# Blocks of half-height matmuls: three pairs side by side instead of two, with the order of VectorE's work changed around them

## The chip, the cores and the metric

One core of one Trainium2 chip. The time is the device time of one execution in microseconds (us), the median of several. Engines: PE is TensorE's matmul, DVE is VectorE, ACT is ScalarE, POOL is GpSimd, SPq is the queue of SyncE that issues the DMAs. "Before" is the tuned kernel, "changed" is the kernel with the change.

## The reference

Two branches read the same normalised input (2048 rows of 448 features), and the output joins them:

```python
def attn(x, wqkv, wo):                 # 16 heads of 28; each row sees 8 rows, 2 apart
    qkv = x @ wqkv
    idx = pos[:, None] - arange(8) * 2
    logits = (q * k[idx]).sum(-1) * 28 ** -0.5       # masked where idx < 0
    return (softmax(logits) * v[idx]).sum() @ wo
def ffn(x, w1, b1, w2, b2):            # 448 -> 1792 -> 448
    return gelu_tanh(x @ w1 + b1) @ w2 + b2
xn  = layernorm(x)
out = x + attn(xn) * silu(ffn(xn))
```

## The kernel before

The rows are worked in four chunks of 512. 448 features are three full contractions of 128 and a "rest" of 64. Two rests, in the upper and the lower 64 rows of the array, run together (0.22 us for the two in the trace of this kernel, as much as one full matmul takes there), so the work comes in pairs: six full matmuls, then two rests (or the rests first). The pairs are seven of the first feed-forward layer (`ps_h`, k = 0 to 6) and four of q/k (`ps_qk`, g = 0 to 3) per chunk. Before, pairs alternate "full, rest" and "rest, full", so that the rests of two neighbours meet in one block:

```python
def ffn1(c, k, even):
    ps = ffn1_tiles(k)
    if even:
        ffn1_full(c, k, ps, True);  ffn1_rest(c, k, ps, False)
    else:
        ffn1_rest(c, k, ps, True);  ffn1_full(c, k, ps, False)
    return ps

def feed_forward_1(c, ps, wos):
    ...
    for k in range(1, MT // 2):
        if (c, k) in ((0, 6), (1, 4), (2, 4)):
            qk_pair(c + 1, 0, True, DD)            # q/k pair 0 of the next chunk
        ps = ffn1(c, k, not odd)
        gelu(k, ps)
        ...
        if k in ((3, 5, 6) if c == 3 else (4,)):   # output projections: ps_s, then sg and o_t on VectorE
            for _ in range(4 if c == 2 else 2):
                if wos: wo_job(wos.pop(0))
        if c and k in (3, 5):                      # tanh on ScalarE, then g on VectorE
            silu_job(4 * (c - 1) + k - 3)
            silu_job(4 * (c - 1) + k - 2)

def ln_apply(t):
    nc.vector.tensor_scalar(xnb[t % 4][:, 0:D], xt(t), mv[:, t, 0:1], rstd[:, t:t + 1], ...)
    nc.vector.tensor_copy(xnb[t % 4][:, D:512], xnb[t % 4][:, D - 64:D])   # doubled features
def ln_dma(t):                                     # tiles 4 to 15: transposed by DMA
    nc.sync.dma_start_transpose(xnT[:, :, LEAD + t * P:LEAD + (t + 1) * P], xnb[t % 4][:, :])
```

`mv` and `rstd` are the mean and the normalising factor of a tile of 128 rows, made from its statistics (`ln_stats`); `rstd` ends just before the tile can be normalised. Two PSUM pools rotate: `psA` (2 tiles of two banks) and `psB` (4 tiles of one bank, shared by q/k, v, `ps_h` of k = 0 and 3, `ps_y`, the output projections and the attention product `psO`). After a chunk's feed-forward pairs come the scores `S`, the other q/k pairs and `psO`, then four more attention units.

The softmax here doesn't subtract the row's maximum and nothing guards it: scores larger than these inputs give would overflow.

## Time and profile before

| | before |
|---|---|
| median (range) | 167.37 us (167.26 to 167.57), 3 runs |
| span of the profiled run | 165.6 us |
| PE, ACT, DVE busy | 158.9, 125.9, 112.9 us |
| stage of chunk 0, 1, 2, 3 | 18.65, 20.66, 22.18, 16.06 us |

A stage, here and below, is the time in PE's timeline from the first `ps_h` matmul of a chunk to the score group after that chunk's first `psO` (in chunk 3, to the next score group). The chain of waits lists pieces of work in order of time (start, length, engine, tile, line); two neighbouring PE pieces whose times join mean that PE never waited. The prediction shows the lines themselves.

### The profile page before, as it was taken

How to read it: one execution, taken by the hardware profiler on the slowest of the kernel's cores; microseconds unless marked ns; L12 is line 12 of the kernel's file. 1: busy time of each engine (PE TensorE's matmuls, PEld its weight loads, DVE VectorE, ACT ScalarE, POOL GpSimd, SP SyncE). 2: the span in 40 equal slices, each digit the busy share in tenths (PEclk: the TensorE clock that was granted, in tenths of full speed). 3: DMA queues.
4: the chain of work that ended last, by engine and by line, in shares of the span. 5: the costliest groups of instructions: out<-in, count | busy, mean ns of one | idle time of the engine just before them, and what ended most of it. 6: DMA issues, size and time to landing. Idle time of an engine off the chain costs nothing.

```text
span 165.6 us, 3242 instructions
## 1 busy us (share of the span) xinstructions
PE 158.9 (96%) x1290; PEld 71.8 (43%) x1301; DVE 112.9 (68%) x256; ACT 125.9 (76%) x198; POOL 4.5 (3%) x16
## 2 busy tenths in 40 slices
PE   6899999999999999999999999999999999999990
PEld 2343333345554334445554334335555334445570
DVE  5967890497888638687888308877777507678893
ACT  3773698598887795998887795698888698698830
POOL 7002000000000000000000000000000000000000
PEclk9999999999999999999999999999999999999999
DMA  5999995520111100100211100300000002020011
GB/s 134 302 306 267 325 190 93 164 44 4 32 36 32 32 0 4 55 0 0 36 32 32 36 0 0 112 1 4 0 4 0 0 0 60 31 83 0 4 55 55
DMA packets 15963, 10.62 MB, mean 64 GB/s; under 512 B 7500, under 2 KB 15948, under 8 KB 15948
## 3 DMA queue, kind: packets, MB, share of 16 engines
q1 hardware_dynamic: 15660, 10.18, 24.0%
q10 hardware_dynamic: 288, 0.23, 0.5%
q8 instruction: 10, 0.16, 0.4%
q14 instruction: 5, 0.04, 0.1%
HBM read 7.00 MB, written 1.84 MB: 53 GB/s over the span
## 4 chain that ended last, share of the span: by engine, by line
PE 83%; ACT 7%; DVE 5%; DMA 2%; issue 1%; DVEq 0%
PE ps_y L281 23%; PE ps_h L249 21%; PE ps_qk L197 11%; PE ps_v L228 8%; PE ps_s L331 6%; PE ps_h L258 4%; PE S L355 3%; PE psO L370 3%; ACT hT L264 3%; PE ps_qk L207 3%; DMA x<-in_A_x_dram 2%; ACT th L310 1%; DVE sg L337 1%; DVE st L161 1%; ACT L509 1%
## 5 line engine op out<-in xcount | busy, mean ns | idle before, releaser
L264 ACT ACTIVATE hT<-ps_h,b1f 128x512 bf16<-128x512 f32 x56 | 34.1, 695 | 10.1 <-PE ps_h L258 7.3
L249 PE MATMUL ps_h<-xnT,w 128*128 128x512 bf16 x161 | 39.3, 380 | 0.5 <-issue 0.2
L281 PE MATMUL ps_y<-w,hT 128*128 128x448 bf16 x196 | 39.5, 353 | 0.0
L361 ACT ACTIVATE E<-S 128x976 bf16<-128x976 f32 x34 | 31.6, 983 | 2.1 <-PE S L355 0.8
L281 PEld LDWEIGHTS <-hT 128*128 128x128 bf16 x196 | 18.0, 98 | 16.7
L249 PEld LDWEIGHTS <-w 128*128 128x128 bf16 x168 | 15.0, 98 | 22.1 <-issue 6.4
L363 DVE TENSOR_TENSOR E<-E,mk_gen 128x976 bf16<-128x976 bf16 x30 | 20.0, 666 | 6.7 <-ACT E L361 6.5
L197 PE MATMUL ps_qk<-xnT,wqk 128*128 128x512 bf16 x92 | 22.2, 380 | 0.3 <-issue 0.2
L379 DVE TENSOR_TENSOR oT<-psO,den 128x484 bf16<-128x484 f32 (+1 forms) x17 | 11.3, 662 | 10.1 <-ACT den L378 10.1
L214 DVE CAST qT<-ps_qk 128x512 bf16<-128x512 f32 x16 | 11.0, 687 | 9.5 <-PE ps_qk L207 8.4
L228 PE MATMUL ps_v<-wv,xnT 128*128 128x448 bf16 x68 | 15.7, 353 | 0.1
L311 DVE SCALAR_TENSOR_TENSOR g<-th,y 128x448 bf16<-128x448 bf16 x13 | 7.6, 621 | 10.8 <-ACT th L310 10.8
L337 DVE SCALAR_TENSOR_TENSOR sg<-ps_s,g 128x448 bf16<-128x448 f32 (+2 forms) x17 | 10.1, 592 | 7.0 <-PE ps_s L331 6.9
L233 ACT CAST vw<-ps_v 128x448 bf16<-128x448 f32 x17 | 9.1, 533 | 6.9 <-PE ps_v L228 6.8
L197 PEld LDWEIGHTS <-wqk 128*128 128x128 bf16 x96 | 8.9, 98 | 11.5 <-issue 1.8
L331 PE MATMUL ps_s<-wo,oT 128*128 128x448 bf16 (+2 forms) x68 | 13.4, 342 | 0.0
L377 ACT ACTIVATE den<-den 128x484 f32<-128x484 f32 (+1 forms) x17 | 10.3, 605 | 4.0 <-DVE den L374 4.0
L374 DVE STREAM_SHUFFLE den<-psO 128x484 f32<-128x484 f32 (+1 forms) x17 | 11.7, 695 | 0.0
L378 ACT ACTIVATE den<-den 128x484 f32<-128x484 f32 (+1 forms) x17 | 10.3, 606 | 0.5
L161 DVE BATCH_NORM_STATS2 st<-x 128x6 f32<-128x448 bf16 x16 | 9.8, 610 | 0.9 <-DMA x<-in_A_x_dram 0.8
L331 PEld LDWEIGHTS <-oT 128*128 128x128 bf16 x68 | 6.4, 98 | 5.9 <-issue 0.2
L228 PEld LDWEIGHTS <-xnT 128*128 128x128 bf16 x68 | 6.3, 98 | 6.0 <-ACT xnT L181 0.6
(71 smaller groups left out, 139.8 us busy)
## 6 DMA issues: line engine op xcount, KB each, us to landing
out_dram<-o_t SPq DMA_DIRECT2D x15, 112.0 KB
w<-in_B_w_dram SPq DMA_DIRECT2D x1, 1568.0 KB
x<-in_A_x_dram SPq DMA_DIRECT2D x3, 448.0 KB
w<-in_B_w_dram SPq DMA_DIRECT2D x2, 672.0 KB
wraw<-in_A_wqkv_dram SPq DMA_DIRECT2D x1, 672.0 KB
w<-in_B_w_dram SPq DMA_DIRECT2D x4, 112.0 KB
wo<-in_A_wo_dram SPq DMA_DIRECT2D x16, 24.5 KB
wv<-in_A_wqkv_dram SPq DMA_DIRECT2D x1, 336.0 KB
```

Source lines behind the costliest of these rows:

```text
L161: nc.vector.bn_stats(out=st[:], in_=xt(t))
L197: nc.tensor.matmul(ps[w][:, :], wqk[:, kt, 16 * w + 4 * g:16 * w + 4 * g + 4, :], xnT[:, kt, LEAD + c * CH:LEAD + (c + 1) * CH], start=(fi ...
L228: nc.tensor.matmul(ps[:, :], xnT[:, kt, o:o + P], wv[:, kt, :], start=(kt == 0), stop=(kt == KT - 1))
L249: nc.tensor.matmul(ps[i][:, :], w1[:, kt, m * P:(m + 1) * P], xnT[:, kt, LEAD + c * CH:LEAD + (c + 1) * CH], start=(first and kt == 0), st ...
L264: nc.scalar.activation(hT[:, m, :], ps[i][:, :], ACT.Gelu_apprx_tanh, bias=b1f[:, m:m + 1])
L281: nc.tensor.matmul(ps[:, :], hT[:, m, tt * P:(tt + 1) * P], w2[:, m, :], start=(m == 0), stop=(m == MT - 1))
L331: nc.tensor.matmul(ps[:, 0:n], oT[:, g, t * P:(t + 1) * P], wo[:, g, cs], start=(g == 0), stop=(g == 3))
L337: nc.vector.scalar_tensor_tensor(out=sg[:, cs], in0=ps[:, 0:cs.stop - cs.start], scalar=0.5, in1=g_sb[t % NG][:, cs], op0=ALU.mult, op1=AL ...
L361: nc.scalar.activation(ev, Sp[p2][:, :, :, 0:QW], ACT.Exp, scale=SCALE)
L363: nc.vector.tensor_tensor(out=ev, in0=ev, in1=mkb, op=ALU.mult)
L374: nc.vector.stream_shuffle(den[:, :, 0:n], psO[:, :, 0:n], [0] * 32)
L379: nc.vector.tensor_tensor(out=oT[:, :, QB * b:QB * b + n], in0=psO[:, :, 0:n], in1=den[:, :, 0:n], op=ALU.mult)
```

## The change

The intent: fewer blocks of rests, since every block costs PE time on entry and exit (about 0.10 us each in the trace of the kernel before; "mode changes" below). Rests of up to three pairs stand side by side where the PSUM banks allow it, the doubled features of the first chunk are made by two 64-wide transposes in the array instead of a copy on VectorE, and one of the last additions goes to GpSimd. The diff is shortened.

```diff
+    def group(*jobs):
+        for job in jobs: job.alloc()
+        jobs[0].full(True)
+        jobs[0].rest(False)
+        for job in jobs[1:]: job.rest(True)
+        jobs[0].done(True)
+        for job in jobs[1:]:
+            job.full(False)
+            job.done(False)
 ...
+        p = [FF1(c, 0, ahead=gelus), FF1(c, 1, then=stats(4 * c + 8)), FF1(c, 2),
+             FF1(c, 3, then=...silus(t)...), FF1(c, 4), FF1(c, 5, then=silus(t + 2)), FF1(c, 6, ...)]
+        group(*p[0:3])
+        if c == 3:
+            group(*p[3:5]); wo_jobs(2); group(*p[5:7]); wo_jobs(4)
+        elif c:
+            group(p[3], *q0)
+            group(*p[4:6])          # ends with tanh and g of k = 5
+            wo_jobs(4)              # 2 projections in chunk 1, 4 in chunk 2
+            group(p[6], *last)      # last = q/k pair 1, and S with q/k pair 2
+        else:
+            group(*p[3:5]); group(p[5], *q0); group(p[6], *last)
 ...
-        for kt in range(KT):
+        for kt in range(3):
             nc.tensor.transpose(pT[:, kt, :], xnb[t % 4][:, kt * P:(kt + 1) * P], ident[:])
+        for r in (0, 64):
+            nc.tensor.transpose(pT[r:r + 64, 3, :], xnb[t % 4][:, D - 64:D], ident[:])
 ...
-        for g in range(4):                     # chunk 0: statistics of tile 4 + g after pair g
-            qk_pair(0, g, g % 2 == 0, DA) ...
+        group(QK(0, 0, DA), QK(0, 1, DA))
+        ln_stats(4); ln_stats(5)
+        group(QK(0, 2, DA), QK(0, 3, DA))
+        ln_stats(6); ln_stats(7)
 ...
-        wo_put(14, s14)
+        wo_put(14, s14, add=nc.gpsimd)
```

Besides, in the start part, v blocks 1 and 3 go to `psA`, the evacuations of the transposes go ahead of those of v, and ten warming matmuls run instead of nine.

More of the change, by code (lines that the diff above doesn't have):

```diff
@@ L166, in ln_rstd, with ln_apply @@
         nc.scalar.activation(rstd[:, t0:t0 + n], lnv[:, t0:t0 + n], ACT.Exp, scale=-0.5)
-    def ln_apply(t):
+    def ln_apply(t, double=True):
         nc.vector.tensor_scalar(xnb[t % 4][:, 0:D], xt(t), mv[:, t, 0:1], rstd[:, t:t + 1],
                                 op0=ALU.subtract, op1=ALU.mult)
-        nc.vector.tensor_copy(xnb[t % 4][:, D:512], xnb[t % 4][:, D - 64:D])
+        if double:
+            nc.vector.tensor_copy(xnb[t % 4][:, D:512], xnb[t % 4][:, D - 64:D])
     def ln_tr(t):
         pT = psB.tile([P, KT, P], BF16, name="pT", tag="B")
-        for kt in range(KT):
+        for kt in range(3):
             nc.tensor.transpose(pT[:, kt, :], xnb[t % 4][:, kt * P:(kt + 1) * P], ident[:])
+        for r in (0, 64):
+            nc.tensor.transpose(pT[r:r + 64, 3, :], xnb[t % 4][:, D - 64:D], ident[:])
         return pT
@@ L192, in qk_weights @@
                               bass.AP(src.tensor, src.offset, [list(src.ap[0]), [DH, H], [1, 32]]))
-    def qk_full(c, g, ps, first, copies):
-        for w in range(2):
-            for kt in range(3):
-                nc.tensor.matmul(ps[w][:, :], wqk[:, kt, 16 * w + 4 * g:16 * w + 4 * g + 4, :],
-                                 xnT[:, kt, LEAD + c * CH:LEAD + (c + 1) * CH],
-                                 start=(first and kt == 0), stop=(not first and kt == 2))
-            if not first:
-                qk_put(c, g, w, ps, copies)
@@ L203, in qk_rest, with __init__, alloc, full @@
-    def qk_rest(c, g, ps, first, copies):
-        for w in range(2):
-            r = slice(64 * w, 64 * w + 64)
-            nc.tensor.matmul(ps[w][:, :], wqk[r, 3, 16 * w + 4 * g:16 * w + 4 * g + 4, :],
-                             xnT[r, 3, LEAD + c * CH:LEAD + (c + 1) * CH], start=first, stop=not first)
-        if not first:
-            for w in range(2):
-                qk_put(c, g, w, ps, copies)
     def qk_put(c, g, w, ps, copies):
         copies[w]((qT, kT)[w][:, g, LEAD + c * CH:LEAD + (c + 1) * CH], ps[w][:, :])
-    def qk_pair(c, g, even, copies):
-        ps = [psB.tile([P, CH], F32, name="ps_qk", tag="B") for _ in range(2)]
-        for f in ((qk_full, qk_rest), (qk_rest, qk_full))[not even]:
-            f(c, g, ps, f is (qk_full, qk_rest)[not even], copies)
+    class QK:
+        def __init__(self, c, g, copies):
+            self.c, self.g, self.copies = c, g, copies
+        def alloc(self):
+            self.ps = [psB.tile([P, CH], F32, name="ps_qk", tag="B") for _ in range(2)]
+        def full(self, first):
+            c, g = self.c, self.g
+            for w in range(2):
+                for kt in range(3):
+                    nc.tensor.matmul(self.ps[w][:, :], wqk[:, kt, 16 * w + 4 * g:16 * w + 4 * g + 4, :],
+                                     xnT[:, kt, LEAD + c * CH:LEAD + (c + 1) * CH],
+                                     start=(first and kt == 0), stop=(not first and kt == 2))
+                if not first:
+                    qk_put(c, g, w, self.ps, self.copies)
+        def rest(self, first):
+            c, g = self.c, self.g
+            for w in range(2):
+                r = slice(64 * w, 64 * w + 64)
+                nc.tensor.matmul(self.ps[w][:, :], wqk[r, 3, 16 * w + 4 * g:16 * w + 4 * g + 4, :],
+                                 xnT[r, 3, LEAD + c * CH:LEAD + (c + 1) * CH], start=first, stop=not first)
+        def done(self, first):
+            if first:
+                for w in range(2):
+                    qk_put(self.c, self.g, w, self.ps, self.copies)
@@ L222, with v_mm @@
+    def group(*jobs):
+        for job in jobs:
+            job.alloc()
+        jobs[0].full(True)
+        jobs[0].rest(False)
+        for job in jobs[1:]:
+            job.rest(True)
+        jobs[0].done(True)
+        for job in jobs[1:]:
+            job.full(False)
+            job.done(False)
     DA, DD = (nc.vector.tensor_copy, nc.scalar.copy), (nc.vector.tensor_copy, nc.vector.tensor_copy)
-    def v_mm(b):
-        ps = psB.tile([P, D], F32, name="ps_v", tag="B")
+    def v_mm(b, pool=psB):
+        ps = pool.tile([P, D], F32, name="ps_v", tag="B" if pool is psB else "A")
@@ L236, in v_job @@
         v_put(b, v_mm(b))
-    def ffn1_tiles(k):
-        if k in (0, 3):
-            return [psB.tile([P, CH], F32, name="ps_h", tag="B") for _ in range(2)]
-        ps = psA.tile([P, 2, CH], F32, name="ps_h", tag="A")
-        return [ps[:, i, :] for i in range(2)]
-    def ffn1_full(c, k, ps, first):
-        for i in range(2):
-            m = 2 * k + i
-            for kt in range(3):
-                nc.tensor.matmul(ps[i][:, :], w1[:, kt, m * P:(m + 1) * P],
-                                 xnT[:, kt, LEAD + c * CH:LEAD + (c + 1) * CH],
-                                 start=(first and kt == 0), stop=(not first and kt == 2))
@@ L253, in ffn1_rest, with __init__, alloc, full @@
-    def ffn1_rest(c, k, ps, first):
-        for i in range(2):
-            m = 2 * k + i
-            r = slice(64 * i, 64 * i + 64)
-            nc.tensor.matmul(ps[i][:, :], w1[r, 3, m * P:(m + 1) * P],
-                             xnT[r, 3, LEAD + c * CH:LEAD + (c + 1) * CH], start=first, stop=not first)
-    def gelu(k, ps):
-        for i in range(2):
-            m = 2 * k + i
-            nc.scalar.activation(hT[:, m, :], ps[i][:, :], ACT.Gelu_apprx_tanh, bias=b1f[:, m:m + 1])
-    def ffn1(c, k, even):
-        ps = ffn1_tiles(k)
-        if even:
-            ffn1_full(c, k, ps, True)
-            ffn1_rest(c, k, ps, False)
-        else:
-            ffn1_rest(c, k, ps, True)
-            ffn1_full(c, k, ps, False)
-        return ps
+    class FF1:
+        def __init__(self, c, k, ahead=lambda: None, then=lambda: None):
+            self.c, self.k, self.ahead, self.then = c, k, ahead, then
+        def alloc(self):
+            if self.k in (0, 3):
+                self.ps = [psB.tile([P, CH], F32, name="ps_h", tag="B") for _ in range(2)]
+            else:
+                ps = psA.tile([P, 2, CH], F32, name="ps_h", tag="A")
+                self.ps = [ps[:, i, :] for i in range(2)]
+        def full(self, first):
+            for i in range(2):
+                m = 2 * self.k + i
+                for kt in range(3):
+                    nc.tensor.matmul(self.ps[i][:, :], w1[:, kt, m * P:(m + 1) * P],
+                                     xnT[:, kt, LEAD + self.c * CH:LEAD + (self.c + 1) * CH],
+                                     start=(first and kt == 0), stop=(not first and kt == 2))
+        def rest(self, first):
+            for i in range(2):
+                m = 2 * self.k + i
+                r = slice(64 * i, 64 * i + 64)
+                nc.tensor.matmul(self.ps[i][:, :], w1[r, 3, m * P:(m + 1) * P],
+                                 xnT[r, 3, LEAD + self.c * CH:LEAD + (self.c + 1) * CH],
+                                 start=first, stop=not first)
+        def done(self, first):
+            self.ahead()
+            for i in range(2):
+                m = 2 * self.k + i
+                nc.scalar.activation(hT[:, m, :], self.ps[i][:, :], ACT.Gelu_apprx_tanh, bias=b1f[:, m:m + 1])
+            self.then()
@@ L333, in wo_mm, with wo_put @@
         return ps
-    def wo_put(t, ps, cs=slice(0, D)):
+    def wo_put(t, ps, cs=slice(0, D), add=nc.vector):
         sg = work.tile([P, D], BF16, name="sg", tag="sg", bufs=3)
@@ L339, in wo_put @@
         o_t = work.tile([P, D], BF16, name="o_t", tag="o_t", bufs=3)
-        nc.vector.tensor_tensor(out=o_t[:, cs], in0=xt(t)[:, cs], in1=sg[:, cs], op=ALU.add)
+        add.tensor_tensor(out=o_t[:, cs], in0=xt(t)[:, cs], in1=sg[:, cs], op=ALU.add)
         nc.sync.dma_start(dram_rows(out_par, t, 1)[:, 0, cs], o_t[:, cs])
@@ L389, in busy, with feed_forward_1, gelus, stats @@
             nc.tensor.matmul(ps[:, :], wz[:, 0:P], wz[:, :], start=True, stop=True)
-    def feed_forward_1(c, ps, wos):
-        nc.scalar.preload_act_table_set(SET_GELU)
-        gelu(0, ps)
-        for k in range(1, MT // 2):
-            if (c, k) in ((0, 6), (1, 4), (2, 4)):
-                qk_pair(c + 1, 0, True, DD)
-            odd = k in {0: (1, 3, 5, 6), 3: (1, 3, 5)}.get(c, (1, 3, 4, 6))
-            ps = ffn1(c, k, not odd)
-            gelu(k, ps)
-            if c + 2 < NC and k in (1, 3):
-                for t in range(4 * c + 7 + k, 4 * c + 9 + k):
-                    ln_stats(t)
-            if k in ((3, 5, 6) if c == 3 else (4,)):
-                for _ in range(4 if c == 2 else 2):
-                    if wos:
-                        wo_job(wos.pop(0))
-            if c and k in (3, 5):
-                silu_job(4 * (c - 1) + k - 3)
-                silu_job(4 * (c - 1) + k - 2)
-        nc.scalar.preload_act_table_set(SET_EXP)
+    def feed_forward_1(c, ahead, wos, last=()):
+        def gelus():
+            ahead()
+            nc.scalar.preload_act_table_set(SET_GELU)
+        def stats(t):
+            def f():
+                if c + 2 < NC:
+                    ln_stats(t)
+                    ln_stats(t + 1)
+            return f
+        def silus(t):
+            def f():
+                if c:
+                    silu_job(t)
+                    silu_job(t + 1)
+            return f
+        def wo_jobs(n):
+            for _ in range(n):
+                if wos:
+                    wo_job(wos.pop(0))
+        q0 = [QK(c + 1, 0, DD)] if c + 1 < NC else []
+        t = 4 * (c - 1)
+        p = [FF1(c, 0, ahead=gelus), FF1(c, 1, then=stats(4 * c + 8)), FF1(c, 2),
+             FF1(c, 3, then=lambda: (stats(4 * c + 10)(), silus(t)())), FF1(c, 4), FF1(c, 5, then=silus(t + 2)),
+             FF1(c, 6, then=lambda: nc.scalar.preload_act_table_set(SET_EXP))]
+        group(*p[0:3])
+        if c == 3:
+            group(*p[3:5])
+            wo_jobs(2)
+            group(*p[5:7])
+            wo_jobs(4)
+        elif c:
+            group(p[3], *q0)
+            group(*p[4:6])
+            wo_jobs(4)
+            group(p[6], *last)
+        else:
+            group(*p[3:5])
+            group(p[5], *q0)
+            group(p[6], *last)
@@ L415 @@
     with tc.manual_schedule(engines={ENG.PE, ENG.Activation, ENG.DVE, ENG.Pool, ENG.SP}):
         nc.scalar.preload_act_table_set(SET_EXP)
-        busy(9)
+        busy(10)
         ln_stats(0)
@@ L421 @@
         ln_rstd(1, 1)
-        ln_apply(0)
+        ln_apply(0, False)
         pT = [ln_tr(0)]
@@ L427 @@
         ln_rstd(2, 1)
-        ln_apply(1)
+        ln_apply(1, False)
         pT.append(ln_tr(1))
@@ L433 @@
         ln_rstd(3, 1)
+        ln_apply(2, False)
+        pT.append(ln_tr(2))
+        v1 = v_mm(1, psA)
+        ln_put(2, pT[2])
         v_put(0, v0)
-        ln_apply(2)
-        pT.append(ln_tr(2))
-        v1 = v_mm(1)
-        ln_put(2, pT[2])
-        v_put(1, v1)
-        ln_apply(3)
+        ln_apply(3, False)
         pT.append(ln_tr(3))
@@ L443 @@
         ln_put(3, pT[3])
+        v_put(1, v1)
+        v3 = v_mm(3, psA)
         v_put(2, v2)
-        v_job(3)
+        v_put(3, v3)
         pb = psB.tile([P, MT], BF16, name="pb", tag="B")
@@ L453 @@
         nc.vector.tensor_copy(b1f[:], pb[:, :])
-        for g in range(4):
-            qk_pair(0, g, g % 2 == 0, DA)
-            if g == 3:
-                ln_stats(7)
-                ln_rstd(4, 4)
-            else:
-                ln_stats(4 + g)
-        ps = ffn1(0, 0, True)
-        for t in range(4, 8):
-            ln_apply(t)
-            ln_dma(t)
-        late_loads()
+        group(QK(0, 0, DA), QK(0, 1, DA))
+        ln_stats(4)
+        ln_stats(5)
+        group(QK(0, 2, DA), QK(0, 3, DA))
@@ new lines, with first_norm, __init__, full @@
+        ln_stats(6)
+        ln_stats(7)
+        ln_rstd(4, 4)
+        def first_norm():
+            for t in range(4, 8):
+                ln_apply(t)
+                ln_dma(t)
+            late_loads()
+        class Scores:
+            def __init__(self, qk, b):
+                self.qk, self.b, self.late = qk, b, []
+                qk.copies = (nc.vector.tensor_copy, lambda *a: self.late.append(a))
+                self.alloc, self.rest, self.done = qk.alloc, qk.rest, qk.done
+            def full(self, first):
+                self.E = qk_unit(self.b, lambda: self.qk.full(first))
@@ L467 @@
         units = iter(range(NB))
+        norm = first_norm
         for c in range(3):
-            feed_forward_1(c, ps, [[], [0, 1], [2, 3, 4, 5]][c])
             n = c + 1
-            qk_pair(n, 1, True, DD)
-            norm = lambda: None
+            b = next(units)
+            sc = Scores(QK(n, 2, None), b)
+            feed_forward_1(c, norm, [[], [0, 1], [2, 3, 4, 5]][c], (QK(n, 1, DD), sc))
+            if n + 1 < NC:
+                ln_rstd(4 * n + 4, 4)
+            nc.scalar.copy(*sc.late[0])
+            group(QK(n, 3, DA))
+            norm = av_unit(b, sc.E)
@@ L473 @@
             vs = iter(range(4 * n, 4 * n + (5 if c == 2 else 4)))
-            for i in range(5):
+            for i in range(1, 5):
                 b = next(units)
-                if i == 0:
-                    tail = []
-                    E = qk_unit(b, lambda: qk_pair(n, 2, False, (nc.vector.tensor_copy, lambda *a: tail.append(a))))
-                    if n + 1 < NC:
-                        ln_rstd(4 * n + 4, 4)
-                    nc.scalar.copy(*tail[0])
-                    qk_pair(n, 3, True, DA)
-                else:
-                    E = qk_unit(b)
-                    norm()
-                    ffn2_job(4 * c + i - 1)
-                    v_job(next(vs))
-                    if n + 1 < NC:
-                        ln_apply(4 * n + 3 + i)
-                        ln_dma(4 * n + 3 + i)
+                E = qk_unit(b)
+                norm()
+                ffn2_job(4 * c + i - 1)
+                v_job(next(vs))
+                if n + 1 < NC:
+                    ln_apply(4 * n + 3 + i)
+                    ln_dma(4 * n + 3 + i)
@@ L491 @@
                 norm = av_unit(b, E)
-            norm()
             for b in vs:
                 v_job(b)
-            ps = ffn1(n, 0, True)
-        feed_forward_1(3, ps, [6, 7, 8, 9, 10, 11])
+        feed_forward_1(3, norm, [6, 7, 8, 9, 10, 11])
         E15 = qk_unit(15)
```

## The prediction

> **What bounds the kernel now.** I read the page first (busy times, clock), then the chain of waits in order of time, then the timelines of PE, ACT and DVE in the feed-forward stage of chunk 1. The page:
>
> ```profile
> PE 158.9 (96%) x1290; PEld 71.8 (43%) x1301; DVE 112.9 (68%) x256; ACT 125.9 (76%) x198; POOL 4.5 (3%) x16
> PEclk9999999999999999999999999999999999999999
> PE 83%; ACT 7%; DVE 5%; DMA 2%; issue 1%; DVEq 0%
> ```
>
> TensorE (PE) is busy from about 5 us to 162 us at full clock and carries the end. So a matmul interval removed is a gain, and any wait put on PE is a loss that nothing later gives back. The chain of waits shows what a group of half-height "rest" matmuls (contraction 64, two side by side) costs:
>
> ```profile
> 17.97 1.29 PE ps_h L249 x6
> 19.26 0.54 PE ps_h L258 x4
> 19.80 2.70 PE ps_h L249 x12
> ...
> 27.67 1.29 PE ps_qk L197 x6
> 28.96 0.32 PE ps_qk L207 x2
> 29.29 0.22 PE ps_h L258 x2
> 29.50 1.40 PE ps_h L249 x6
> ...
> 32.52 0.33 PE S L355 x16
> 32.85 0.32 PE ps_qk L207 x2
> ```
>
> Six full matmuls take 1.29 (0.216 each), but 1.40 after rests; two rests take 0.22 beside rests, but 0.32 as the first of a block. So entering and leaving a block cost about 0.10 each, and a further pair costs 0.226 in a block. The score group S (L355) is in yet another shape: rests next to it pay 0.10 as well.
>
> In the stage of chunk 1 (PE starts it at 53.1) the chain leaves PE:
>
> ```profile
> 64.56 1.24 PE ps_h L249 x5
> 65.81 0.34 PE ps_h L258 x2
> 66.15 0.02 issue
> 66.17 1.27 ACT hT L264 x2
> 67.44 0.93 ACT th L310 x2
> 68.37 1.17 ACT hT L264 x2
> 69.53 0.04 issue
> 69.58 0.39 PE S L355 x14
> ```
>
> S waits there for the last two gelus (in PE's timeline its 16 matmuls span 0.67, in chunk 0 only 0.39), and the following psO group lasts 0.54 instead of 0.34 because it waits for the masked exponentials: 0.49 of PE waiting in chunk 1, and the same in chunk 2. Last, VectorE (DVE) in that stage:
>
> ```profile
> 64.84 0.62 DVE L337 SCALAR_TENSOR_TENSOR sg<-ps_s,g 128x448 bf16<-128x448 f32 x1
> 65.49 0.39 DVE L340 TENSOR_TENSOR o_t<-x,sg 128x448 bf16<-128x448 bf16 x1
> 65.80 0.62 DVE L337 SCALAR_TENSOR_TENSOR sg<-ps_s,g 128x448 bf16<-128x448 f32 x1
> 66.45 0.39 DVE L340 TENSOR_TENSOR o_t<-x,sg 128x448 bf16<-128x448 bf16 x1
> 67.94 1.16 DVE L311 SCALAR_TENSOR_TENSOR g<-th,y 128x448 bf16<-128x448 bf16 x2 [1.09 <-ACT th L310]
> ```
>
> Here the output projections are evacuated (sg) before the second pair of g, which waits for the tanh of ScalarE (ACT). That order matters below.
>
> [...]
>
> **The change part by part.** All from intervals above, in us; negative is a gain.
>
> *Mode changes.* Chunk 0's q/k pairs keep two blocks. Per chunk 0, 1, 2 the stage has four two-pair blocks, then q/k pair 1 (rests), S, pair 2 (rests first), pair 3 (rests), psO: 8 + 6 changes. After: blocks of (0,1,2), two of two pairs, one of (6, pair 1, pair 2), then S between full matmuls, pair 3, psO: 8 + 4. Saved: one entry 0.096, one exit 0.107, 0.009 at S, less 2 x 0.010 for the longer blocks: 0.19. Chunk 3: four blocks become three: 0.20. Pure PE gain 3 x 0.19 + 0.20 = 0.77.
>
> *Chunk 0.* ACT is nearly tied with PE at psO: from the last gelus to the masked E it needs 5.18 (30.94 to 36.12). After, k=6 ends 13.01 after the stage's start and psO cannot start before 18.2, PE would be there at 18.13; before it was 18.31. Gain 0.1.
>
> *Chunks 1 and 2: a new wait.* Two things move. The second tanh pair goes out of the stretch just before S (good: it would remove most of the 0.49). But the output projections now follow the group (4,5), and the tanh and g of k=5 are issued ahead of them, so on DVE both g stand in front of the sg. The four PSUM banks rotate: the rests of q/k pair 2, now pulled ahead of S, write the banks that the projections hold. The waits in the built program say so: in chunk 1 the two rests of pair 2 wait for the two sg; in chunk 2 the four rests of pairs 1 and 2 wait for the four sg.
> Chunk 1, from the stage's start: PE does group (0,1,2) in 4.76, (3, pair 0) to 7.99, (4,5) to 11.23, eight projections (8 x 0.189) to 12.74, k=6 and its rests, the pair 1 rests, and wants the pair 2 rests at 14.58. The gelus of k=5 can start when PE has finished it: 11.42. From there, by the before trace, the two g end 2.92 later (66.17 to 69.10): 14.34; sg at 14.26 to 14.88, o_t, second sg 15.22 to 15.84. So PE waits until about 15.89: 1.30. Then pair 1 to 17.51, S at 17.60, pairs 2 and 3, psO at 20.95, next S at 21.32; before, that S came at 20.65 (73.78 less 53.13). Loss 0.67. (Check: 1.30 - 0.19 - 0.49 + rounding.)
> Chunk 2: projections 16 x 0.189, pair 2's rests wanted at 16.10; the fourth sg ends 2 x 0.96 later than the second: 17.76. PE waits 1.71. psO at 22.87, next S at 23.21; before 22.18. Loss 1.03.
>
> *Chunk 3.* S at 15.86 instead of 16.06; the banks' sg are early enough. Gain 0.20.
>
> *Start.* Four copies of 0.18 leave DVE, but steps of about 0.21 per tile only help until ACT binds: evacuation of the first transpose, rstd, evacuation follow each other on ACT. The two 64-wide transposes add a mode change (about 0.1) per tile before that. What helps is that the evacuations of transposes 2 and 3 are no longer behind v evacuations. I put v of block 3 at 10.11 instead of 10.36: gain 0.25. The wqk copies (from 9.99, waiting for their load) allow it. The later stats order delays rstd by 0.34, and the load by transposing DMA to 27.27 where PE needs it at 27.42: hidden, just.
>
> *Tail.* DVE's o_t (0.39) for tile 14 leaves the last chain; without a collision the last o_t comes 0.29 earlier. [...] and the queue issues outputs in order, so tile 14's store holds the last two. I take +0.1.
>
> Sum: -0.1 + 0.67 + 1.03 - 0.20 - 0.25 + 0.1 = +1.25: 167.37 + 1.25 = 168.6.
>
> **Rivals.** *A: the wait does not bite.* If g and sg are faster or PE reaches the rests later, the gain is 0.77 of mode changes, 0.8 of removed waits, 0.25 at the start, some at the end: 165.7. For it: PE's 96% and the intent. Against: the gelus of k=5 start from a PE event, and the chain of 4.4 behind it is measured. I give it one in ten. *B: GpSimd at the end costs more.* If the addition takes 2 us instead of 1, the last stores slip by another 1: 169.4. Against: its small ops here take 0.23 to 0.43. *C: start or chunk 0 slip* because of the transposing DMA: up to 0.3 more. *D: only mode changes matter*, all else hidden: 166.6.
>
> **Range and chances.** Chunks 1 and 2 sum to +1.7 with perhaps 0.5 of doubt, start and tail 0.4 each: 167.5 to 169.4 holds eight in ten, the rest mostly rival A. 2% is 3.35 us; A gains half of that and the known losses reach 1.9 with everything bad: faster 0.01, within 2% 0.96, slower 0.03.
>
> **What would show it.** Chunk 1: the rests of pair 2 stand about 1.3 behind those of pair 1, and about 1.7 in chunk 2, released by DVE sg; S there no longer waits for gelus. Rest blocks (in the chain: pieces of rests with no full matmuls between) fall from 27 to 20. PE busy time hardly moves. Start: first q/k matmul near 11.1 instead of 11.33. Tail: the GpSimd addition near 1 us[...]. I am wrong if PE has no gap before S in chunks 1 and 2.

Passages are cut, and marked. The sum is +1.25 and so 168.6. Its last term, the tail's +0.1, was chosen between 0.29 earlier and a later end; without that term the sum is +1.15, or 168.5. The 1 us that the forecast and rival B give GpSimd's addition stands without its working; the runs show 1.03.

## The result, and the profile after

| | before | changed |
|---|---|---|
| median (range), 6 runs each | 167.47 us (167.03 to 167.77) | 169.34 us (169.12 to 169.75) |
| span of the profiled run | 165.6 us | 167.6 us |

The ratio is 1.0114 (95 % interval 1.0094 to 1.0134). A ratio, here and below, is the mean time of one kernel's fast runs over that of the other's in the same rounds, so not quite the ratio of the medians. Within 2 % this counts as the same; in microseconds the change costs 1.9.

By stages, from PE's timelines (us):

| piece | before | changed | difference | predicted |
|---|---|---|---|---|
| start, to the first feed-forward matmul | 17.81 | 17.63 | -0.18 | -0.25 |
| stage of chunk 0 | 18.65 | 19.24 | **+0.59** | **-0.1** |
| stage of chunk 1 | 20.66 | 21.27 | +0.61 | +0.67 |
| stage of chunk 2 | 22.18 | 23.19 | +1.01 | +1.03 |
| stage of chunk 3 | 16.06 | 15.85 | -0.21 | -0.20 |
| from `psO` of unit 15 to the last `o_t` | 10.79 | 10.89 | +0.10 | +0.1 |

With 0.02 from rounding and the stretches between, the differences sum to +1.94, against +1.25 predicted. Five terms lie within 0.1 us of the prediction and one, chunk 0, does not.

The page of the changed kernel, its engine line and its chain line:

```profile
PE 158.9 (95%) x1295; PEld 72.2 (43%) x1306; DVE 112.4 (67%) x251; ACT 125.7 (75%) x198; POOL 5.6 (3%) x17
PE 78%; DVE 12%; ACT 5%; issue 2%; DMA 1%; SPq 0%; DVEq 0%
```

PE is as busy as before, but its share of the chain falls from 83 % to 78 % and VectorE's rises from 5 % to 12 %: the chain now leaves PE for VectorE. The chain of waits shows where:

```profile
25.34 2.42 DMA xnT<-xnb
...
27.90 0.39 PE ps_qk L222 x2
...
66.73 0.50 DVE g L329
67.27 0.62 DVE g L329
67.89 0.55 DVE sg L355
68.46 0.39 DVE o_t L358
68.85 0.55 DVE sg L355
69.44 0.37 PE ps_qk L222
...
108.64 0.63 DVE sg L355
109.31 0.37 PE ps_qk L222
```

In chunk 0, PE's rests of the next chunk's q/k pair 0 start 0.14 us after the fourth transposing DMA has landed. In chunks 1 and 2 the chain runs through both g, then sg, o_t, sg, and then the rests of q/k pair 2. PE's timeline in chunk 1 (start, length, line, shapes, count, idle time before and what ended it) shows the wait as two gaps:

```profile
67.89 0.38 PE L222 MATMUL ps_qk<-xnT,wqk 64*128 64x512 bf16 x2
68.47 0.37 PE L222 MATMUL ps_qk<-xnT,wqk 64*128 64x512 bf16 x1 [0.20 <-DVE sg L355]
69.44 0.37 PE L222 MATMUL ps_qk<-xnT,wqk 64*128 64x512 bf16 x1 [0.59 <-DVE sg L355]
```

The line at 67.89 holds the rests of pair 1. The last rest of pair 2 starts 1.55 us later. It would come 0.23 later if nothing held it (a pair costs that in a block), and measured from matmul start to matmul start the wait is 1.31 us; in chunk 2, by the same reading, 1.72. The records overlap (in the kernel before, that of two rests at 28.90 is 0.39 long and the next rests start 0.22 after it), so the gaps that the timeline prints are smaller than the waits.

The tail: GpSimd's addition and VectorE's o_t beside it in the changed kernel, first GpSimd's timeline, then VectorE's,

```profile
162.99 1.03 POOL L358 TENSOR_TENSOR o_t<-x,sg 128x448 bf16<-128x448 bf16 x1 [150.29 <-DVE sg L355]
```

```profile
163.36 0.86 DVE L358 TENSOR_TENSOR o_t<-x,sg 128x336 bf16<-128x336 bf16 x1
```

and the same o_t before, in VectorE's timeline:

```profile
161.94 0.33 DVE L340 TENSOR_TENSOR o_t<-x,sg 128x336 bf16<-128x336 bf16 x1
```

The addition took 1.03 us, and o_t took 0.86 instead of 0.33: it ended 0.20 us after GpSimd had.

### The profile page after: what moved, and what is told of

Same layout as the page of the kernel before. It is cut to its first block, busy times and chain, and to the rows that moved or that the text cites. A ratio compares the mean times of both kernels' runs of the same rounds, so it can differ in the third digit from the quotient of the medians.

```text
span 167.6 us, 3250 instructions
## 1 busy us (share of the span) xinstructions
PE 158.9 (95%) x1295; PEld 72.2 (43%) x1306; DVE 112.4 (67%) x251; ACT 125.7 (75%) x198; POOL 5.6 (3%) x17
## 4 chain that ended last, share of the span: by engine, by line
PE 78%; DVE 12%; ACT 5%; issue 2%; DMA 1%; SPq 0%; DVEq 0%
PE ps_y L299 23%; PE ps_h L276 16%; PE ps_qk L212 12%; PE ps_v L249 8%; PE S L373 3%; PE ps_h L284 3%; PE psO L388 3%; DVE sg L355 3%; PE ps_w L407 3%; PE ps_s L349 3%; PE ps_qk L222 2%; DVE st L161 2%; DVE g L329 2%; ACT hT L292 2%; DMA xnT<-xnb 1%
## 5 line engine op out<-in xcount | busy, mean ns | idle before, releaser
L276 PEld LDWEIGHTS <-w 128*128 128x128 bf16 x168 | 15.5, 98 | 21.1 <-issue 3.8
L212 PEld LDWEIGHTS <-wqk 128*128 128x128 bf16 x96 | 8.4, 98 | 13.5 <-issue 4.7
```

The lines of the kernel that those rows point to most:

```text
L212: nc.tensor.matmul(self.ps[w][:, :], wqk[:, kt, 16 * w + 4 * g:16 * w + 4 * g + 4, :], xnT[:, kt, LEAD + c * CH:LEAD + (c + 1) * CH], star ...
L276: nc.tensor.matmul(self.ps[i][:, :], w1[:, kt, m * P:(m + 1) * P], xnT[:, kt, LEAD + self.c * CH:LEAD + (self.c + 1) * CH], start=(first a ...
```

## The experiments

The theory to be tried: (1) in chunks 1 and 2 PE waits because g, which waits for tanh, stands in front of sg on VectorE while the rests of q/k pair 2 need the banks that sg frees; (2) in chunk 0 PE waits for the transposing DMA, because the statistics of tiles 4 to 7 are issued later; (3) the GpSimd addition holds VectorE. The main rival of all three is that the longer blocks of rests, or the changed start, cost the time themselves. Each run was timed against the kernel before on the same chip; each result was correct.

### g after sg

```diff
-   FF1(c, 5, then=silus(t + 2)),
+   FF1(c, 5, then=silus(t + 2) if c == 3 else lambda: None),
 ...
    group(*p[4:6])
    wo_jobs(4)
+   silus(t + 2)()
    group(p[6], *last)
```

> The changed kernel, except that in chunks 1 and 2 the second pair of tanh and g is issued after the output projections and their sg, not before them. Theory (g stands in front of sg on VectorE and the banks of the projections come free late): the PE waits of 1.31 us (chunk 1) and 1.72 us (chunk 2) before the rests of q/k pair 2 go, both stages end 1.3 and 1.7 us earlier, about 0.7 us below the kernel before, and the time falls by 3.0 us to about 166.3. Rival (the projections or the longer rest blocks hold PE by themselves): PE still waits more than 0.5 us in front of those rests and the time falls by less than 1 us.

Measured: 166.29 us, ratio 0.9936 (0.9917 to 0.9956). The stage of chunk 1 takes 20.08 us, that of chunk 2 21.59, so 1.19 and 1.60 below the changed kernel and 0.58 and 0.59 below the kernel before. PE's timeline in chunk 1:

```profile
67.49 0.39 PE L284 MATMUL ps_h<-xnT,w 64*128 64x512 bf16 x2
67.71 0.59 PE L222 MATMUL ps_qk<-xnT,wqk 64*128 64x512 bf16 x4
68.24 1.47 PE L212 MATMUL ps_qk<-xnT,wqk 128*128 128x512 bf16 x6
```

The four rests of pairs 1 and 2 run without a gap, between the rests of k = 6 and the next full matmuls. VectorE in the same stretch:

```profile
66.51 0.62 DVE L355 SCALAR_TENSOR_TENSOR sg<-ps_s,g 128x448 bf16<-128x448 f32 x1
...
67.47 1.15 DVE L329 SCALAR_TENSOR_TENSOR g<-th,y 128x448 bf16<-128x448 bf16 x2
```

The second sg is done at 67.13, before the rests want its bank; g comes after. No work was taken away; in each of the two chunks, two instructions on VectorE and two on ScalarE changed places. The stages fell by 0.1 less than the waits that went (1.31 and 1.72), because a little of an old wait came back: psO lasts 0.45 us instead of the 0.33 in the changed kernel (0.54 in the kernel before); in chunk 1 the last of its masked exponentials ends at 73.06, after psO has begun (72.99). The theory for chunks 1 and 2 holds, and the rival (longer blocks cost by themselves) falls: with the blocks as they are, both stages are shorter than before.

### The statistics between the q copies again

```diff
-   group(QK(0, 0, DA), QK(0, 1, DA)); ln_stats(4); ln_stats(5)
-   group(QK(0, 2, DA), QK(0, 3, DA)); ln_stats(6); ln_stats(7)
+   group(QK(0, 0, DA, st(4)), QK(0, 1, DA, st(5)))     # st(t): ln_stats(t) after that pair's copies
+   group(QK(0, 2, DA, st(6)), QK(0, 3, DA, st(7)))
```

> The changed kernel, except that the statistics of tiles 4 to 7 stand between the q copies of chunk 0 again, one after each pair, as in the kernel before. Theory (the grouped order of the statistics delays rstd by 0.38 us and with it the transposing DMA, for which PE waits 0.67 us at the rests of chunk 1's q/k pair 0): rstd comes 0.3 to 0.4 us earlier, the wait falls to 0.3 us or less, and the time falls by 0.4 to 0.7 us to 168.6 to 168.9. Rival (the transfers are late because they run beside the bulk load of the weights, which the earlier start brings them nearer to): rstd comes earlier but the landing moves by under 0.2 us, and the time stays within 0.2 us of 169.3.

Measured: 169.05 us, ratio 1.0098 (1.0077 to 1.0119), not told apart from the changed kernel's 1.0114 by the intervals. In the profile, rstd ends 1.92 us after the stage's start, as before (1.92), where the changed kernel had 2.29. But the rests of q/k pair 0 still wait for the DMA and start at 27.77 instead of 27.90 (10.04 us after the stage's start instead of 10.27), and the stage still takes 19.01 us. Even the 0.23 between 19.01 and 19.24 is not clear of what this wait varies by itself: two more profiles with the changed kernel's code up to here show 19.28 (g after sg) and 19.07 (the addition on VectorE, below). So my theory (2) was about a third of the truth at most: the first normalised rows come as early as before, and the transfers still land late. The rival, that they run beside the bulk load, stood, and had to be tried by itself.

### The load of w2 after the transposing DMAs

```diff
-   nc.sync.dma_start(w2[:, :, :], B_w2...)      # with the first loads
    def late_loads():                            # issued after the DMAs of tiles 4 to 7
+       nc.sync.dma_start(w2[:, :, :], B_w2...)
```

> The changed kernel, except that the 1.6 MB load of w2 is issued after the four transposing DMAs of tiles 4 to 7, not before them, so that no bulk load runs beside them. Theory (the transfers compete with the bulk load): the four issues take about 5.2 us in all instead of 5.9, PE's wait of 0.67 us at the rests of chunk 1's q/k pair 0 falls under 0.2 us, and the time falls by 0.5 to 169.0 or less against 169.3. Rival (the issuing of the transposing DMAs is slow by itself: about 1.3 us each after the first normalised row, whatever else runs): last issue still 4.6 us or more behind the first, wait still 0.4 us or more, time within 0.2 us of the changed kernel.

Measured: 168.57 us, ratio 1.0071 (1.0052 to 1.0091). The stage of chunk 0 takes 18.59 us, 0.06 less than before, where the prediction had 0.1 less. The DMA queue's line in the changed kernel, then in this one:

```profile
20.65 5.91 SPq L187 DMA_TRANSPOSE xnT<-xnb  x4
```

```profile
20.73 5.23 SPq L187 DMA_TRANSPOSE xnT<-xnb  x4
26.01 0.58 SPq L134 DMA_DIRECT2D w<-in_B_w_dram  x1
```

The four issues take 5.23 us instead of 5.91, with the grouped statistics left as the change has them, and PE doesn't wait. The bulk load beside the transposing DMAs is what made PE wait.

### The start part alone

The kernel before with only the start part of the change (the two 64-wide transposes, the pools of v, the evacuation order).

```diff
-   for kt in range(KT):
+   for kt in range(3):
        nc.tensor.transpose(pT[:, kt, :], ...)
+   for r in (0, 64):
+       nc.tensor.transpose(pT[r:r + 64, 3, :], xnb[t % 4][:, D - 64:D], ident[:])
 ...    # pools of v and order of evacuations as in the change
```

> The kernel before with the start part of the change alone: doubled features by two 64-wide transposes, v blocks 1 and 3 in the other pool, evacuations in the changed order, 10 warming matmuls. Theory: the first q/k matmul comes 0.15 to 0.25 us earlier against the end of the loads and everything behind it too, no new DMA wait: the time falls by 0.2 us to about 167.1. Rival (the transposing DMAs end at a fixed moment set by the loads): PE waits up to 0.2 us in chunk 0 and the time stays at 167.3.

Measured: 167.51 us, ratio 1.0008 (0.9987 to 1.0029): the rival. From the end of the first rstd (4.72 us) to the first feed-forward matmul (17.34) it takes 12.62 us instead of 12.77, a gain of 0.15, but the stage of chunk 0 takes 19.22 us instead of 18.65. With the statistics in the old order and no three-pair block anywhere, PE waits for the same DMA (the queue's line, and PE's):

```profile
19.98 6.30 SPq L187 DMA_TRANSPOSE xnT<-xnb  x4
```

```profile
27.62 1.46 PE L200 MATMUL ps_qk<-xnT,wqk 128*128 128x512 bf16 x6 [0.42 <-DMA xnT<-xnb]
```

The queue began 0.47 us earlier than before (20.45) and the four issues took 0.6 us longer (6.30 against 5.70). Whatever the start gained, the load beside it took back.

### The start part with the late w2, and its control

The start part alone, plus the late load of w2 as above; then the kernel before with the late load alone.

```diff
    # in either: the load of w2 in late_loads(), as above
```

> The kernel before with the start part alone and the load of w2 after the four transposing DMAs. Theory (the start part gains 0.15 us from the first statistics to the first feed-forward matmul, and the start part alone lost it again to the wait for the transposing DMA beside the bulk load): no DMA wait, chunk 0's stage 18.65 us as before instead of 19.22, time 0.15 to 0.5 us below the start part alone, 167.0 to 167.3. Rival (the start part gains nothing by itself): chunk 0's stage falls but the time stays that of the kernel before within 0.1 us, 167.4.

Measured: 166.95 us, ratio 0.9978 (0.9957 to 1.0000). Stage of chunk 0: 18.65 us, no DMA wait; first rstd to first feed-forward matmul 12.61.

> The kernel before with the load of w2 after the four transposing DMAs and nothing else; the control for the version with the start part and the late w2 (ratio 0.9978). Theory (in the kernel before PE does not wait for the transposing DMA, so taking the bulk load away gains nothing): chunk 0's stage 18.65 us as before, time within 0.1 us of the kernel before, so the 0.2 to 0.4 us of the other version are the start part's. Rival (the late w2 itself pays, for instance because the early loads land sooner): 0.2 us or more below the kernel before.

Measured: 167.10 us, ratio 0.9981 (0.9964 to 0.9997). Its profile agrees with the kernel before in every stage within 0.02 us, as the theory says, but its time is lower by some 0.3 us, as the rival says. The early loads did not land sooner in the profile (first rstd at 5.05 against 5.04), and its six runs (167.07 to 167.33) lie at the lower edge of those of the kernel before (167.10 to 167.74). What makes the upper part of those runs go is open. So the total of the version with the start part can't be credited to the start part; what is shown of it is the 0.15 us in the profile.

The transposing DMAs together, from the queue's lines and the packets of the trace (us; some versions come below; "wait" is chunk 0's stage above the same kernel's stage without the load beside it: 18.65 with the old groups, 18.59 with the new):

| kernel | w2 load beside | first issue | four issues took | first issue to last packet | wait |
|---|---|---|---|---|---|
| before | yes | 20.45 | 5.70 | 6.46 | 0 |
| start part alone | yes | 19.98 | 6.30 | 7.05 | 0.57 |
| changed | yes | 20.65 | 5.91 | 6.66 | 0.65 |
| changed, g after sg | yes | 20.43 | 5.95 | 6.71 | 0.69 |
| changed, addition on VectorE | yes | 20.80 | 5.74 | 6.50 | 0.48 |
| changed, statistics between | yes | 20.37 | 6.07 | 6.82 | 0.42 |
| all three mends | yes | 20.15 | 6.21 | 6.96 | 0.57 |
| before, late w2 | no | 20.45 | 5.25 | 6.01 | 0 |
| changed, late w2 | no | 20.73 | 5.23 | 5.99 | 0 |
| start part, late w2 | no | 20.03 | 5.23 | 5.99 | 0 |

Without the load, 6.0 us; with it, 6.5 to 7.05, and among those with the new start the longer the earlier the queue begins. The changed kernel, "g after sg" and "addition on VectorE" run the same code up to the end of this stage, so 0.48 to 0.69 is how far the wait varies by itself. In the kernel before, PE needed the rows just after they came (wanted at 27.67, the last semaphore of the fourth DMA at 27.35).

The traces also tell what the load slows. In all fourteen profiles the last packet comes 0.75 or 0.76 us after the last issue has ended, so what delays the last rows is the issuing. One issue alone is stretched: without the load the first takes 1.3 us and the others 1.2 each; with it, the first takes 1.82 to 2.38 with the new start, and in the kernel before the second takes 1.67 (with its blocks single, the first: 1.85). In the seven profiles with the new start and the load, that first issue ends between 22.27 and 22.64 us, wherever between 19.98 and 20.80 it began: what begins earlier only waits longer there. What holds the issue until then is not shown.

### The addition on VectorE, and on GpSimd alone

```diff
-   wo_put(14, s14, add=nc.gpsimd)      # the changed kernel
+   wo_put(14, s14)
```

> The changed kernel, except that the closing addition of tile 14 is on VectorE again. Theory (the GpSimd addition holds VectorE's o_t of tile 15[...], 0.86 instead of 0.33 us): that o_t takes 0.33 us again, tile 14's addition takes 0.39 us on VectorE, and the time falls by 0.1 to 0.3 us. Rival (the addition on GpSimd really relieves the last chain): the last o_t ends later and the time rises by about 0.3 us.

Measured: 169.17 us, ratio 1.0110 (1.0089 to 1.0130), not told apart from the changed kernel in time. In VectorE's timeline o_t takes 0.33 again:

```profile
163.76 0.33 DVE L358 TENSOR_TENSOR o_t<-x,sg 128x336 bf16<-128x336 bf16 x1
```

The tail takes 10.79 us instead of 10.89. The other way round, in the kernel before:

> The kernel before with one thing alone changed: the closing addition of tile 14 on GpSimd. Theory: GpSimd takes 1.0 us for it, VectorE's o_t of tile 15 that lies beside it grows from 0.33 to about 0.9 us, and the time rises by 0.1 to 0.3 us over the kernel before. Rival (a gain of the 0.39 us that leaves VectorE): the time falls by 0.2 to 0.4 us.

Measured: 167.46 us, ratio 1.0006 (0.9986 to 1.0026). GpSimd takes 1.03 us, o_t beside it 0.86, and the tail 10.89 instead of 10.79. Moving the addition costs 0.10 us in the tail, both ways; the totals can't resolve it.

### Blocks of single pairs

To price a block of rests by itself: the kernel before with every pair's full matmuls ahead of its own rests, 44 blocks instead of 27.

```diff
-   ps = ffn1(c, k, not odd)
+   ps = ffn1(c, k, True)
 ...
-   qk_pair(0, g, g % 2 == 0, DA)
+   qk_pair(0, g, True, DA)
```

> The kernel before with every pair's full matmuls ahead of its own rests, so that no two pairs share a block of rests: 44 blocks instead of 27. Theory (each block costs an entry and an exit of 0.10 us, on PE's path): 17 blocks more at 0.2 us, 3.4 us if PE never waits otherwise; as PE waits 0.5 us in chunks 1 and 2 anyway, 2.4 to 3.4 us slower, 170 to 171 us. Rival (a block costs next to nothing[...]): within 0.5 us of the kernel before.

Measured: 170.34 us, ratio 1.0172 (1.0148 to 1.0196), 2.9 us. The start grew by 0.41 us for 2 more blocks (measured from the first rstd), chunk 0 by 0.85 for 4, chunk 1 and 2 by 0.62 each for 4, chunk 3 by 0.64 for 3: 3.14 for 17, 0.18 us a block, and 0.21 in the stages where PE does not wait for anything else. PE's timeline in chunk 1:

```profile
57.42 0.39 PE L258 MATMUL ps_h<-xnT,w 64*128 64x512 bf16 x2
57.74 1.47 PE L249 MATMUL ps_h<-xnT,w 128*128 128x512 bf16 x6
59.14 0.39 PE L258 MATMUL ps_h<-xnT,w 64*128 64x512 bf16 x2
```

From rest to rest 1.72 us: six full matmuls (1.29), two rests (0.22), and 0.21 for one entry and one exit. The rival falls; the idea of the change was sound.

### All three mends

g after sg, the statistics between the copies, the addition on VectorE.

```diff
    # the edits of "g after sg", "The statistics between" and "The addition on VectorE" together
```

> The changed kernel with all three mends at once: g after sg in chunks 1 and 2, the statistics of tiles 4 to 7 between the q copies, the closing addition on VectorE. Theory (the three costs lie in different stages and add up): the gains of the single mends, 3.0, 0.3 and 0.15 us as measured against the changed kernel's 169.3, sum to 3.4, so 165.9 us, 0.4 us below the version with the first mend alone; PE still waits about 0.3 us for the transposing DMA in chunk 0. Rival (the mends after the first hide in one another): 166.3, no better than the first alone.

Measured: 166.12 us, ratio 0.9925 (0.9905 to 0.9944); expected 165.9. Stages 19.16, 20.08, 21.58, 15.85, tail 10.79. The miss is in chunk 0, where the wait stayed at 0.57 us, as the table above leads one to expect of an early start beside the load. In time it is not told apart from the first mend alone.

### Two ways out of the wait in chunk 0

Either q/k pair 0 is wanted later:

```diff
-   group(p[5], *q0); group(p[6], *last)
+   group(*p[5:7]);   group(*q0, last[0])       # chunk 0
 ...
+   E = qk_unit(b, lambda: group(q/k pair 2, q/k pair 3))
```

> All three mends, and in chunk 0 the q/k pair 0 of chunk 1 is taken out of the group with the sixth pair of feed-forward: groups (3,4), (5,6), then (q/k 0, q/k 1), S, (q/k 2, q/k 3). The number of rest blocks is the same, but PE needs the transposed rows about 1.7 us later. Theory (PE waits in chunk 0 for the transposing DMA and nothing else): the wait goes, chunk 0's stage falls by 0.4 us or more below that of the version with the three mends, and the time by as much, to about 165.5. Rival (the gelus and exponentials of ScalarE bind the end of that stage anyway): the first attention product starts no earlier and the time is that of the three mends.

Measured: 165.81 us, ratio 0.9906 (0.9889 to 0.9923). The DMA wait is gone, but the stage of chunk 0 takes 18.91 us, only 0.25 below the three mends: `psO` now spans 0.71 us instead of 0.45, waiting for the masked exponentials of VectorE. Half theory, half rival.

Or the load is moved, with the groups as in the change:

```diff
    # the three mends, and the load of w2 in late_loads()
```

> All three mends, and the load of w2 after the four transposing DMAs; the groups stay as in the change. Theory (the wait for the transposing DMA in chunk 0, 0.43 us with the three mends, is made by the bulk load beside it): the wait goes, chunk 0's stage takes 18.5 to 18.6 us instead of 19.16, and the time falls by 0.5 from the 166.1 of the three mends to about 165.6. Rival (with the wait gone ScalarE's chain binds the stage): 19.0 us and no change in time.

Measured: 165.60 us (165.49 to 166.12), ratio 0.9898 (0.9877 to 0.9920); chunk 0's stage 18.55 us. PE's rests of q/k pair 0, in the changed kernel and then in this one, from PE's timelines:

```profile
27.90 0.39 PE L222 MATMUL ps_qk<-xnT,wqk 64*128 64x512 bf16 x2 [0.51 <-DMA xnT<-xnb]
```

```profile
27.03 0.38 PE L222 MATMUL ps_qk<-xnT,wqk 64*128 64x512 bf16 x2
```

That is 10.27 us after the stage's start in the changed kernel (17.63), and 9.60 here (17.43): this is when PE wants the rows if nothing holds it. The engine line of its page:

```profile
PE 157.7 (96%) x1295; PEld 72.1 (44%) x1306; DVE 112.5 (69%) x252; ACT 125.6 (77%) x198; POOL 4.5 (3%) x16
```

This beats both kernels: 1.0 % below the kernel before in the same rounds (within 2 %, so by that measure still the same). Of that, the 0.2 % that the late load alone gave the kernel before is not explained. It keeps every block and the start of the change, with the order of VectorE and of the queue put right.

## Why the prediction was right or wrong

The time, 168.6 us, was 0.7 below the measured 169.34, which lies just inside the range: nearly the whole miss is one term, chunk 0.

- *Mode changes, -0.77 in all.* Right where they can be read alone. The blocks of rests fell from 27 to 20, as forecast. Chunk 3, where nothing else changed, gained 0.21 against 0.20 predicted. The single blocks give 0.18 to 0.21 per block.
- *Chunks 1 and 2, the new wait.* Right in mechanism and size: waits of 1.31 and 1.72 against 1.30 and 1.71, stages +0.61 and +1.01 against +0.67 and +1.03 (the 0.67 is 0.05 more than its own check gives, 1.30 - 0.19 - 0.49 = 0.62, which is what came). The order on VectorE was the cause, as the first experiment shows. Without the wait the stages gain 0.58 and 0.59, where the same working (0.19 of mode changes and 0.49 of removed waits) gives 0.68; the rest is the wait at psO.
- *Start, -0.25.* Right in sign, smaller: from the end of the first rstd to the first feed-forward matmul it is 12.61 us in the changed kernel, 12.77 before, a gain of 0.15. The shortfall is already in the step that the prediction named: v of block 3 starts 0.14 earlier after the first rstd (5.17 against 5.31), not 0.25. It can be read only from that interval, since the first rstd itself ends between 4.72 and 5.05 us from run to run. Six of the ten profiles with the new start show 12.61 or 12.62; in the other four, 12.69 to 12.99, the third rstd came 0.2 to 0.5 us later after the first. The mode change that it put at about 0.1 per tile is two such steps in the changed kernel's trace (tile 3): from the third transpose to the 64-wide ones 0.15 us, where the others start 0.06 apart, and from these to v 0.18, where it was 0.06; from the first transpose to v it is 0.44 instead of 0.22.
- *Chunk 0, -0.1.* This is the step that failed, in the words of the prediction: "the load by transposing DMA to 27.27 where PE needs it at 27.42: hidden, just". The rows landed at 27.76, 0.49 later, PE wanted them at 27.23, 0.19 earlier, and it waited about 0.65 us: +0.59 instead of -0.1.
  - When PE wants them: 27.42 fits the place of q/k pair 0 in the chain of the kernel before (27.67) less the 0.25 of the start. There its full matmuls come first; the new block asks for its rests first. By the prediction's own pieces (two blocks to 7.99, six full matmuls 1.29, two rests 0.32) that is 9.60 us after the stage's start, as the last version shows, and 27.16 with the start that it forecast: ahead of its own landing.
  - When they land: counted from the stage's start, the first issue came 0.38 later than in the kernel before (3.02 against 2.64; the prediction had 0.34 for rstd), and the four issues took 0.21 longer (5.91 against 5.70). The prediction took the transfers' own time from the kernel before. The runs show that time to depend on what runs beside: 6.0 us without the load of w2, 6.5 in the kernel before, 6.66 in the changed one and 7.05 in the earliest start. How it came to 27.27 is not shown either: in the trace of the kernel before the last semaphore of the fourth DMA comes at 27.35, which with its own +0.34 and -0.25 gives 27.44.

  Rival C, "up to 0.3 more", named the place and sized it at half or less. With the load out of the way the term itself was right: 18.59 us, -0.06.
- *Tail, +0.1.* Right: +0.10, in both directions of the test. But it was picked between 0.29 earlier and a later end, so that it fits so closely is luck. The addition took 1.03 us on GpSimd, and o_t beside it 0.86 instead of 0.33, in either kernel. That o_t is held until the addition ends was not shown: it ended 0.20 us after the addition, less than the 0.33 that it takes alone, and why it takes longer beside the addition is open. The queue did issue the last three stores in order: that of tile 14 at 164.05, just after the addition's end (164.02), and the next at 164.47, 0.25 after its o_t had ended (164.22); the last was not held (its o_t ended at 165.03, it was issued at 165.05).
- *Rival A* (the wait does not bite, 165.7; its terms 0.77, 0.8 and 0.25 give 165.55) is about what the mended version reaches (165.60), since it has no wait, though with the late load besides; as a forecast for the change as written it was rightly put at one in ten. *Rival B* (169.4; 1 us on top of 168.6 would be 169.6) falls: the addition took 1.03 us, not 2, and that the time came close to 169.4 has another cause. *Rival D* falls too: chunks 1 and 2 did not only gain mode changes.

Still open: what holds the one stretched issue of the transposing DMAs while the load runs, and why the kernel before with only the late w2 ran 0.3 us faster with an unchanged profile.

## What to carry to other kernels

When work is pulled forward on the bounding engine, list the buffers that it writes and ask when their last reader on the other engines is done; here two g in front of the sg of two chunks cost about 3 us, and changing places gave them back. The margin of 0.15 us under the transposing DMAs was none beside a bulk load: the four took 6.0 us without the load of w2 and 6.5 to 7.05 with it. Ask of a transfer's time from a profile what ran beside it there, and remember that the moment at which its data are wanted moves with the order too (here 0.19 earlier than forecast). Price a mode change by adding some (here 17 blocks, 3.14 us in the stages), and compare stages rather than totals when one part is worth less than the runs' spread.
